# One access pattern for two, a stage buffer in other memory, and a planner with measured matmul times

## The chip, the cores and the metric

The kernel runs on one core of one Trainium2 chip. The metric is the device time of one execution in microseconds, lower is better; the time before is the median of three runs. A core has five engines that run instruction streams of their own: TensorE (PE in the profile; its weight loads are PEld), VectorE (DVE), ScalarE (ACT), GpSimd (POOL) and SyncE (SP), which here only issues transfers. Transfers between the on-chip memory (SBUF) and the chip's main memory (HBM) are moved by 16 DMA engines. Matmul results go to PSUM, which has eight banks.

## The reference

Two branches read the same kind of 2048 x 512 token matrix and are mixed by a gate for each token:

```
g = sigmoid(sum(u * gate_w))                     # one number per token
P = exp((A * dt) * l),  K = 2 * Re(sum_n C * dt * P)      # 512 channels, 128 states, 2048 positions
a = causal convolution of u with K over 2048 positions (by FFT of length 4096) + u * D_skip
b = ((x @ w_gate) * (x @ w_up)) @ w_down         # 512 -> 1792 -> 512, no other nonlinearity
out = g * a + (1 - g) * b
```

All of it is float32. The kernel writes each matmul of branch b as three products of two-part numbers (high and low part), which keeps float32 accuracy.

## The kernel before, in words

**Branch b (the GLU)** is the larger part of TensorE's work. The 1792 hidden features are 14 blocks of 128, taken in five groups; the 2048 tokens are four chunks of 512. For each group and chunk, `hidden` makes `pg` and `pu` (tokens times `w_gate` and `w_up`, 24 matmuls for a block: two tiles, four depth blocks, three parts), VectorE and ScalarE multiply them and split the result into `hh` and `hl`, and `down` multiplies by `w_down` into `y`. `evacuate` scales `y` by the gate and adds it to the output in HBM by accumulating transfers on GpSimd's queue. The token tiles `x` are split once, kept in HBM as `x_d` and loaded again for later groups.

**Branch a (the convolution)** goes by quarters of 128 channels. VectorE and ScalarE build tables for 32 channels at a time (16 blocks `b`); `k_block` turns a block into kernel values on TensorE (`k<-v,x`). After four blocks, `k_first` does the first stage of the transform of the kernel in two halves `h`: 16 to 48 matmuls into four PSUM banks (`k<-kt`), copies into two stage tiles and two 512 KB writes to the HBM array `s_d`. Then `transforms(q)`: `m_load` reads `s_d` back in another layout, `m_second`, `m_product` and `m_inverse` do the second stage, the product of the spectra and the first inverse stage, written to `y_d`, in four parts T; `m_last` reads `y_d` and does the last inverse stage (`k<-ev`), and `finish` gates the result and adds it to the output. For the last quarter (`q == KT - 1`) the tile is loaded by other code (`v<-y_d`), and the result of its last chunk is added on chip in `ends`.

`m_last` needs, for each of two halves of 16 columns, a tile of 128 partitions with 16 x 128 numbers each (8 KB): row `2k + c` of `y_d[q]` goes to partition `64c + k`. Before, two transfers do it, one for each c.

**Buffers.** Stage tiles come from the tag `ts` of the pool `mid`, three buffers of 4 KB a partition, given out in the order in which the plan asks. The tag `x` of the pool `tab` has two buffers of 8 KB a partition; it holds the tables of two blocks and, at the end, loaded inputs of the last quarter.

**The order of the work** is not that of the program text. Every piece is entered as a task with an engine, a planned duration in us, the tiles that it reads and writes, a rank and, for transfers, a size in KB (`dma=`). `Work.run` then simulates all engines: it always takes the task that can start first (on equal terms, the lower rank), gives out buffers when their last users end, and charges transfers to one bus at 320 KB per us (1024 is 3.2 us). The result is a fixed order of instructions for each engine. GLU products have rank 2, so they fill what the transforms leave. All instructions go through one wrapper, so the profile shows them all at line 102; tiles tell them apart.

Of the kernel before, what the change touches and what calls it, by code (L numbers as in the profile page):

```python
# [18 lines left out]
P = 128  # L19
L, D, N, F = 2048, 512, 128, 1792  # L20
KT = D // P
# [266 lines left out]
def gated_mix_kernel(  # L288
# [20 lines left out]
    add = work.add  # L309
# [224 lines left out]
    def product(pg, which, w, x, kt, after):  # L534
        base = which * D + kt * P

        def fn():
            for n, (a, b) in enumerate(THREE):
                pe.matmul(
                    pg.t, w[a].t[:, base : base + P], x.t[:, b * D : b * D + D], start=kt == 0 and n == 0, stop=kt == KT - 1 and n == 2  # L540
                )

        add("pe", 0.681, fn, r=[(w[0], which), (w[1], which), x], w=[pg], rank=2, after=after)

    steps = []

# [34 lines left out]
    def down(y, r, h, w, first, last):  # L581
        def fn():
            for n, (a, b) in enumerate(THREE):
                pe.matmul(
                    y.t, h[a].t[:, r * P : (r + 1) * P], w[b].t, start=first and n == 0, stop=last and n == 2
                )

        add("pe", 0.681, fn, r=[*h, *w], w=[y], rank=2)

    ending, stored = [], set()  # L590

# [106 lines left out]
    def u_part(c):  # L698
        ci, r0 = c // 2, c % 2
        ut = inp([P, 2, D])  # L700
        rows_u = uv.rearrange("p (c s r) d -> p c s r d", s=2, r=2)[:, ci, :, r0, :]
        add("sp", 0.42, lambda: sp.dma_start(ut.t, rows_u), w=[ut], dma=512, after=9.0 + 15.0 * c)
        fs = new("mid", "y", [P, 2, D], bufs=2)

        def score_of(j):
            r = 4 * ci + 2 * j + r0
            add(
                "dve", 0.77,
                lambda: dve.scalar_tensor_tensor(
                    fs.t[:, 0], ut.t[:, j, :], 1.0, gw[0].t[:, 2], op0=ALU.mult, op1=ALU.mult,  # L710
                    accum_out=score[:, r : r + 1],
                ),
                r=[ut, (gw[0], 2)], w=[(fs, 0), (m_gate, ("s", ci))], rank=0,
            )

        def fold(to, part, op):
            add(
                "dve", 0.69, lambda: dve.tensor_tensor(out=to(), in0=ut.t[:, 0], in1=ut.t[:, 1], op=op),
                r=[ut], w=[part], rank=0,
            )  # L720

        banks = [bank() for _ in range(4)]
        sts = [stage([P, 2, D]) for _ in range(2)]
        halves = [lambda: fs.t[:, 1], lambda: ut.t[:, 0]]

        def fn():
            for c, src in enumerate(halves):
                for g in range(4):
                    lanes = slice(32 * g, 32 * g + 32)
                    pe.matmul(  # L730
                        banks[g].t[64 * c : 64 * c + 64], w1_t[lanes, 64 * c : 64 * c + 64], src()[lanes],
                        start=True, stop=True, tile_position=(32 * g, 64 * c),
                    )

        for j in range(2):
            score_of(j)
        fold(halves[0], (fs, 1), ALU.add)
        fold(halves[1], (ut, 0), ALU.subtract)
        add("pe", 1.1, fn, r=[ut, fs, m_w1], w=banks, rank=1, hold=sts)
        for g in range(4):  # L740
            st, h, n2 = sts[g // 2], g % 2, 8 * g + c
            add("act", 0.59, lambda h=h, g=g, st=st: act.copy(st.t[:, h], banks[g].t), r=[banks[g]], w=[(st, h)])
            add(
                "pool", 1.7,
                lambda h=h, n2=n2, st=st: [
                    pool_q.dma_start(
                        s_d[:, :, c, n2, 0].rearrange("q k d -> k q d"),
                        st.t[64 * c : 64 * c + 64, h].rearrange("p (f d) -> p f d", f=KT),
                    )
                    for c in range(2)  # L750
                ],
                r=[(st, h)], w=[(m_su, n2)], dma=256,
            )
        if c % 2:
            cs = slice(4 * ci, 4 * ci + 4)
            sc, ga = (m_gate, ("s", ci)), (m_gate, ci)
            add("act", 1.5, lambda: act.activation(score[:, cs], score[:, cs], AF.Tanh, scale=0.5), r=[sc], w=[sc], rank=0)

            def gates():
                dve.tensor_scalar(ngate[:, cs], score[:, cs], -0.5, 0.5, op0=ALU.mult, op1=ALU.add)  # L760
                dve.tensor_scalar(gate[:, cs], score[:, cs], 0.5, 0.5, op0=ALU.mult, op1=ALU.add)

            add("dve", 0.4, gates, r=[sc], w=[ga], rank=0)
# [273 lines left out]
    def k_block(b, x, v):  # L1037
        pk = bank()

        def kgen():  # L1040
            pv = pk.t.rearrange("p (g j) -> p g j", j=64)
            for d in range(TB):
                ch, g = d % 4, d // 4
                for c in range(2):
                    pe.matmul(
                        pv[32 * ch : 32 * ch + 32, g, :], x.t[:, c, d, :], v.t[:, c, d, :], start=c == 0, stop=c == 1,
                        tile_position=(0, 32 * ch),
                    )

        if b % 4 == 0:  # L1050
            kts["now"] = new("tab", "kt", [P, 64, 32])
        kt, g0 = kts["now"], b % 4 * 8
        add("pe", 2.15, kgen, r=[x, v], w=[pk], rank=0, hold=[kt], many=True)
        add(
            "act", 1.09,
            lambda: act.copy(
                kt.t[:, :, g0 : g0 + 8].rearrange("p n g -> p g n"), pk.t.rearrange("p (g j) -> p g j", j=64)
            ),
            r=[pk], w=[(kt, b % 4)],
        )  # L1060
        if b % 4 == 3:
            k_first(b // 4, kt)

    def k_first(q, kt):

        tt(0.19, lambda: kt.t[:, 48, :], lambda: kt.t[:, 48, :], lambda: skip[:, q], ALU.add, [m_skip], [kt])
        for h in range(2):
            banks, sts = [bank() for _ in range(4)], [stage([P, 8, 4, 32]) for _ in range(2)]

            def fn(h=h, banks=banks):  # L1070

                to = 0
                for first, n, second in K_COLS[h]:
                    for b in range(2):
                        n0 = (first, second)[b]
                        for c in range(4):
                            lanes = slice(32 * c, 32 * c + 32)
                            pe.matmul(
                                banks[c].t[:, 32 * to : 32 * (to + n)], w1k_t[lanes, b],
                                kt.t[lanes, n0 : n0 + n, :].rearrange("p n g -> p (n g)"),  # L1080
                                start=b == 0, stop=b == 1, tile_position=(32 * c, 0),
                            )
                    to += n

            add("pe", 2.08, fn, r=[kt, m_w1k], w=banks, rank=-1, hold=sts)
            for half in range(2):

                st = sts[half]
                for c in range(4):
                    cs = slice(256 * half, 256 * half + 256)  # L1090
                    evict(
                        q, c, 0.4, lambda c=c, st=st: st.t[:, :, c, :],
                        lambda c=c, banks=banks, cs=cs: banks[c].t[:, cs].rearrange("p (n g) -> p n g", g=32),
                        [banks[c]], [(st, c)],
                    )
                n0 = 16 * h + 8 * half
                add(
                    "sp", 0.42,
                    lambda n0=n0, st=st: sp.dma_start(
                        s_d[q].rearrange("k c n u d -> (k c) n u d")[:, n0 : n0 + 8, 1],  # L1100
                        st.t.rearrange("p n c g -> p n (c g)"),
                    ),
                    r=[st], w=[(m_sk, (q, n0))], dma=512,
                )

    def evict(q, n, us, to, src, r, w):
# [51 lines left out]
    def m_second(q, ins, w):  # L1158
# [18 lines left out]
                            )  # L1177

        src = [(t, k) for t, k, _ in ins]
        add("pe", 1.85, fn, r=[*src, w], w=banks[0] + banks[1], rank=1, hold=[to])  # L1180
        for i in range(2):
            for e in range(2):
                bk = banks[i][e]
# [40 lines left out]
    def m_inverse(q, T0, ys, ws):  # L1224
# [14 lines left out]
                                    ys[t].t[lanes, k, i, e], start=k == 0, stop=k == 1, tile_position=(32 * j, 64 * e),  # L1239
                                )  # L1240

        add("pe", 2.13, fn, r=[*ys, *(w for w, _ in ws)], w=banks, rank=1, hold=sts, many=True)
        for j in range(4):
            st, m = sts[j // 2], j % 2
            evict(
# [16 lines left out]
    def m_last(q):  # L1262
# [3 lines left out]
        for half in range(2):  # L1266
# [6 lines left out]
            if end:  # L1273
# [2 lines left out]
            t = new("mid", "ev", [P, 16, P], bufs=2)  # L1276
            rows_y = y_d[q].rearrange("(k c) (h n) d -> h c k (n d)", c=2, h=2)[half]
            add(
                "sp", 0.84,
                lambda t=t, rows_y=rows_y: [  # L1280
                    sp.dma_start(t.t[64 * c : 64 * c + 64].rearrange("p n d -> p (n d)"), rows_y[c]) for c in range(2)
                ],
                r=[(m_y, (q, T)) for T in range(4)], w=[t], dma=1024,
            )
            src.append(t)
            rhs.append(lambda t=t: t.t)
# [11 lines left out]
                            start=True, stop=True, tile_position=(64 * c, 32 * g),  # L1298
                        )

        add("pe", 1.6, fn, r=src, w=banks[0] + banks[1], rank=1, hold=fins[0] + fins[1])
        for half in range(2):
            finish(q, half, banks[half], fins[half])

# [170 lines left out]
```

## Time and profile before

| | |
|---|---|
| median of 3 runs | 618.01 us (614.53 to 618.51) |
| profiled execution, its own time | 617.16 us |
| span of the profile | 615.4 us |
| mean granted TensorE clock | 0.991 |
| TensorE busy | 594.9 us (97%) |
| VectorE busy | 514.4 us (84%) |
| ScalarE busy | 405.8 us (66%) |
| transfers | 136.22 MB, mean 221 GB/s |

In the profile's groups, `k<-ev,w_t` is an output tile and the two inputs of a matmul; `x32` counts instructions. In the chain that ended last each row is start, length and what ran or was waited for. In a table by stages the columns are the stretch, its length, the busy time and count of PE, PEld, DVE, ACT and POOL, then the granted clock, the busy share of the 16 DMA engines and GB/s. In a list of transfers each row has the tiles, the queue, how often, the size of one, and the median time from issue to landing.

### The profile page before, as it was taken

Reading aid. Unit: us, or ns where it says so; the run is one execution under the profiler, and the core shown is the slowest. Engines: PE = TensorE matmul, PEld = TensorE weight load, DVE = VectorE, ACT = ScalarE, POOL = GpSimd, SP = SyncE. Lnnn points to the kernel's source line nnn. Section 1 sums busy time; section 2 is a strip of 40 time slices with the busy share of each in tenths; the row PEclk is TensorE's granted clock in tenths of the full one; section 3 lists DMA queues with packets and bytes.
Section 4 is the critical chain, followed back from the end, with each engine's and each line's share of the span. In section 5 each row is a group of like instructions: output and inputs, shape, how many; then the busy total and the mean of one; then the engine's idle time right before and its main releaser. Section 6 shows DMA issues by size and latency. Waiting matters only on the chain.

```text
span 615.4 us, 16233 instructions
## 1 busy us (share of the span) xinstructions
PE 594.9 (97%) x6628; PEld 454.8 (74%) x6628; DVE 514.4 (84%) x813; ACT 405.8 (66%) x923; POOL 106.4 (17%) x165
## 2 busy tenths in 40 slices
PE   8989999999899999999999999899999999999993
PEld 5767777777778877787777788568877787777772
DVE  6967999999989999999999999785999972547725
ACT  5568868776778778678789748575796463464320
POOL 0153433331221102020121011120101011130201
PEclk9999999999999999999999999899999999999997
DMA  8699968657968979399999869397888569798956
GB/s 266 183 359 308 300 235 299 185 138 216 272 183 209 274 249 276 120 257 251 292 207 230 227 209 211 78 191 156 249 225 240 178 180 240 208 289 199 214 131 120
DMA packets 102223, 136.22 MB, mean 221 GB/s; under 512 B 7300, under 2 KB 68228, under 8 KB 101124
## 3 DMA queue, kind: packets, MB, share of 16 engines
q1 hardware_dynamic: 80788, 100.57, 53.0%
q0 software_dynamic: 20672, 34.35, 27.4%
q8 instruction: 52, 0.85, 0.5%
q10 hardware_dynamic: 688, 0.26, 0.2%
q14 instruction: 23, 0.19, 0.1%
HBM read 77.75 MB, written 57.41 MB: 220 GB/s over the span
## 4 chain that ended last, share of the span: by engine, by line
PE 84%; DVE 7%; DMA 4%; issue 2%; ACT 2%; DVEq 0%; SPq 0%; ACTq 0%
PE pg L102 22%; PE pu L102 22%; PE y L102 21%; PE k L102 18%; DMA in<-in_u 2%; DVE x L102 2%; DMA x<-x_d 1%; DVE v L102 1%; DVE y L102 1%; DMA ev<-in_wts 1%; DVE ts L102 1%; ACT acc L102 1%; DMA out<-acc 0%; DVE hl L102 0%; DVE h L102 0%
## 5 line engine op out<-in xcount | busy, mean ns | idle before, releaser
L102 PE MATMUL pg<-x,whi 128*128 128x512 f32 x440 | 137.5, 392 | 1.0 <-ACT whi L102 0.9
L102 PE MATMUL pu<-x,whi 128*128 128x512 f32 x440 | 137.0, 391 | 0.0
L102 POOL DMA_DIRECT2D out<-acc x52 | 44.6, 917 | 331.7 <-ACT acc L102 300.5
L102 PEld LDWEIGHTS pg<-x,whi 128*128 128x128 f32 x440 | 82.9, 188 | 19.8 <-ACT whi L102 2.4
L102 PEld LDWEIGHTS pu<-x,whi 128*128 128x128 f32 x440 | 82.9, 188 | 18.9 <-issue 1.9
L102 PE MATMUL y<-dhi,hl 128*128 128x512 f32 x224 | 91.1, 407 | 0.7 <-ACT acc L102 0.4
L102 PE MATMUL pg<-x,wlo 128*128 128x512 f32 x220 | 88.1, 401 | 1.8 <-DMA x<-x_d 1.1
L102 PE MATMUL pu<-x,wlo 128*128 128x512 f32 x220 | 87.9, 400 | 1.6 <-issue 1.6
L102 PE MATMUL y<-dlo,hh 128*128 128x512 f32 x224 | 87.6, 391 | 0.0
L102 PE MATMUL y<-dhi,hh 128*128 128x512 f32 x224 | 87.4, 390 | 0.0
L102 DVE TENSOR_TENSOR h<-pu,h 128x512 f32<-128x512 f32 x55 | 37.9, 689 | 36.1 <-PE pu L102 32.0
L102 ACT CAST hh<-h 128x512 fp32r<-128x512 f32 x56 | 34.8, 621 | 42.8 <-DVE h L102 42.6
L102 ACT ACTIVATE acc<-y,ngate 128x512 f32<-128x512 f32 x68 | 46.0, 688 | 25.6 <-PE y L102 19.3
L102 ACT COPY ts<-k 128x512 f32<-128x512 f32 (+1 forms) x116 | 48.4, 503 | 21.4 <-PE k L102 21.4
L102 ACT COPY h<-pg 128x512 f32<-128x512 f32 x55 | 32.4, 589 | 42.5 <-PE pg L102 29.5
L102 PEld LDWEIGHTS y<-dhi,hl 128*128 128x128 f32 x224 | 42.0, 187 | 21.9 <-issue 7.7
L102 PEld LDWEIGHTS pg<-x,wlo 128*128 128x128 f32 x220 | 41.4, 188 | 17.6 <-issue 4.3
L102 PEld LDWEIGHTS pu<-x,wlo 128*128 128x128 f32 x220 | 41.4, 188 | 14.2 <-issue 4.9
L102 PEld LDWEIGHTS y<-dhi,hh 128*128 128x128 f32 x224 | 42.1, 188 | 9.3
L102 PEld LDWEIGHTS y<-dlo,hh 128*128 128x128 f32 x224 | 42.1, 188 | 7.6
L102 POOL DMA_DIRECT2D s_d<-ts x64 | 39.6, 626 | 36.0 <-ACT ts L102 28.1
L102 DVE TENSOR_TENSOR hl<-h,hh 128x512 fp32r<-128x512 f32 x56 | 38.4, 686 | 5.0 <-ACT hh L102 4.8
(115 smaller groups left out, 1011.9 us busy)
## 6 DMA issues: line engine op xcount, KB each, us to landing
x<-x_d SPq DMA_DIRECT2D x32, 512.0 KB, 6.5
out<-acc POOLq DMA_DIRECT2D x52, 256.0 KB, 6.4
in<-s_d SPq DMA_DIRECT2D x24, 512.0 KB, 6.1
raw<-in_wts SPq DMA_DIRECT2D x36, 256.0 KB, 4.3
x_d<-x POOLq DMA_DIRECT2D x16, 512.0 KB, 6.4
s_d<-ts POOLq DMA_DIRECT2D x64, 128.0 KB, 5.7
s_d<-ts SPq DMA_DIRECT2D x16, 512.0 KB, 5.9
y_d<-ts SPq DMA_DIRECT2D x16, 512.0 KB, 6.3
```

What stands on the lines that cost most here:

```text
L102: got = getattr(self.engine, name)(*args, **kw)
```

## The change

It does three things.

- In `m_last`, the two 64-partition transfers of one tile become one transfer into all 128 partitions. The planned size goes from 1024 to 1200 and the planned issue time from 0.84 to 0.42 us.
- In `k_first`, the second half of the last quarter stages its copies in one tile of the tag `x` (the two halves of it in place of two `ts` tiles).
- Planned durations of TensorE tasks change; the instructions in them do not.

```diff
-        add("pe", 0.681, fn, r=[(w[0], which), (w[1], which), x], w=[pg], rank=2, after=after)
+        add("pe", 0.684, fn, r=[(w[0], which), (w[1], which), x], w=[pg], rank=2, after=after)
...
-        add("pe", 0.681, fn, r=[*h, *w], w=[y], rank=2)
+        add("pe", 0.684, fn, r=[*h, *w], w=[y], rank=2)
...
-        add("pe", 1.1, fn, r=[ut, fs, m_w1], w=banks, rank=1, hold=sts)
+        add("pe", 1.26, fn, r=[ut, fs, m_w1], w=banks, rank=1, hold=sts)
...
-        add("pe", 2.15, kgen, r=[x, v], w=[pk], rank=0, hold=[kt], many=True)
+        add("pe", 2.24, kgen, r=[x, v], w=[pk], rank=0, hold=[kt], many=True)
...
-            banks, sts = [bank() for _ in range(4)], [stage([P, 8, 4, 32]) for _ in range(2)]
+            banks = [bank() for _ in range(4)]
+            if h and q == KT - 1:
+                pair = new("tab", "x", [P, 2, 8, 4, 32], bufs=2)
+                sts = [((pair, i), lambda i=i: pair.t[:, i]) for i in range(2)]
+            else:
+                sts = [(st, lambda st=st: st.t) for st in (stage([P, 8, 4, 32]) for _ in range(2))]
...
-            add("pe", 2.08, fn, r=[kt, m_w1k], w=banks, rank=-1, hold=sts)
+            add("pe", 2.17, fn, r=[kt, m_w1k], w=banks, rank=-1, hold=[st for st, _ in sts])
...
-                st = sts[half]
+                st, st_at = sts[half]
+                piece = lambda c, st=st: (st, c) if not isinstance(st, tuple) else (st[0], (st[1], c))
...
-                    r=[st], w=[(m_sk, (q, n0))], dma=512,
+                    r=[piece(c) for c in range(4)], w=[(m_sk, (q, n0))], dma=512,
...
-        add("pe", 1.85, fn, r=[*src, w], w=banks[0] + banks[1], rank=1, hold=[to])
+        add("pe", 2.11, fn, r=[*src, w], w=banks[0] + banks[1], rank=1, hold=[to])
...
-        add("pe", 2.13, fn, r=[*ys, *(w for w, _ in ws)], w=banks, rank=1, hold=sts, many=True)
+        add("pe", 2.25, fn, r=[*ys, *(w for w, _ in ws)], w=banks, rank=1, hold=sts, many=True)
...
             rows_y = y_d[q].rearrange("(k c) (h n) d -> h c k (n d)", c=2, h=2)[half]
             add(
-                "sp", 0.84,
-                lambda t=t, rows_y=rows_y: [
-                    sp.dma_start(t.t[64 * c : 64 * c + 64].rearrange("p n d -> p (n d)"), rows_y[c]) for c in range(2)
-                ],
-                r=[(m_y, (q, T)) for T in range(4)], w=[t], dma=1024,
+                "sp", 0.42,
+                lambda t=t, rows_y=rows_y: sp.dma_start(t.t.rearrange("p n d -> p (n d)"), rows_y),
+                r=[(m_y, (q, T)) for T in range(4)], w=[t], dma=1200,
             )
...
-        add("pe", 1.6, fn, r=src, w=banks[0] + banks[1], rank=1, hold=fins[0] + fins[1])
+        add("pe", 2.12, fn, r=src, w=banks[0] + banks[1], rank=1, hold=fins[0] + fins[1])
```

More of the change, by code (lines that the diff above doesn't have):

```diff
@@ L1091, in k_first @@
                     evict(
-                        q, c, 0.4, lambda c=c, st=st: st.t[:, :, c, :],
+                        q, c, 0.4, lambda c=c, st_at=st_at: st_at()[:, :, c, :],
                         lambda c=c, banks=banks, cs=cs: banks[c].t[:, cs].rearrange("p (n g) -> p n g", g=32),
-                        [banks[c]], [(st, c)],
+                        [banks[c]], [piece(c)],
                     )
@@ L1098, in k_first @@
                     "sp", 0.42,
-                    lambda n0=n0, st=st: sp.dma_start(
+                    lambda n0=n0, st_at=st_at: sp.dma_start(
                         s_d[q].rearrange("k c n u d -> (k c) n u d")[:, n0 : n0 + 8, 1],
-                        st.t.rearrange("p n c g -> p n (c g)"),
+                        st_at().rearrange("p n c g -> p n (c g)"),
                     ),
-                    r=[st], w=[(m_sk, (q, n0))], dma=512,
+                    r=[piece(c) for c in range(4)], w=[(m_sk, (q, n0))], dma=512,
                 )
```

## The prediction

> **What bounds the kernel now.** I read the page first, engine shares and the forty slices, then the summary of the chain that ended last.
>
> ```profile
> span 615.4 us, 16233 instructions
> ...
> PE 594.9 (97%) x6628; PEld 454.8 (74%) x6628; DVE 514.4 (84%) x813; ACT 405.8 (66%) x923; POOL 106.4 (17%) x165
> ...
> PE   8989999999899999999999999899999999999993
> ...
> DMA packets 102223, 136.22 MB, mean 221 GB/s; under 512 B 7300, under 2 KB 68228, under 8 KB 101124
> ...
> PE 84%; DVE 7%; DMA 4%; issue 2%; ACT 2%; DVEq 0%; SPq 0%; ACTq 0%
> ```
>
> TensorE is busy 594.9 of 615.4 us and makes up 84% of the chain. It runs its instructions in one fixed order, so whatever its next instruction waits for is paid nearly in full: there is almost no idle time to take it back from. Only 20.5 us are idle. The table by stages says where half of that is:
>
> ```profile
> 600.00:606.00 6.00, 5.17 (x22) 3.62 (x20) 5.79 (x10) 0.59 (x1) 2.24 (x2) 1.00 0.02 1
> 606.00:612.00 6.00, 0.00 (x0) 0.00 (x0) 2.32 (x7) 0.00 (x0) 0.63 (x1) 0.66 1.31 213
> 612.00:615.40 3.40, 0.00 (x0) 0.00 (x0) 0.00 (x0) 0.00 (x0) 0.00 (x0) 0.50 0.49 166
> ```
>
> 9.4 us at the end and some 0.8 us before it are a tail of VectorE and stores. The other 10 us are spread over the start and the middle.
>
> **The change, part by part.**
>
> *The plan's constants.* No instruction changes. Seven TensorE costs rise: 656 products by 0.003 us, then 8 by 0.16, 16 by 0.09, 8 by 0.09, 16 by 0.26, 8 by 0.12 and 4 by 0.52, together 12.6 us that the plan did not know of. They change only the order in which work is issued. The gain is at most the 10 us of idle above; a loss of the same size is possible. I take 0, between -4 and +8.
>
> *The second half of the last kernel stage.* Before, it needs two of three "ts" buffers, and the first half still holds two of them until its writes have landed. The chain and the SP queue in that stretch:
>
> ```profile
> 509.03 1.93 PE k L102 x16
> ...
> 526.15 1.97 PE k L102 x48
> ...
> 534.49 1.88 PE k L102 x32
> ```
> ```profile
> 511.85 7.31 SPq L102 DMA_DIRECT2D s_d<-ts  x2
> ...
> 529.00 1.33 SPq L102 DMA_DIRECT2D s_d<-ts  x2
> ...
> 534.91 0.93 SPq L102 DMA_DIRECT2D v<-s_d  x2
> ```
>
> The halves are 17.1 us apart on TensorE, and GLU products fill the gap. With table buffers the second half can follow as soon as the first half's four banks are copied out, some 13 us earlier. Its two writes still go down the same transfer queue as everything before them. At the rate of that stretch (500 to 545), two 512 KB writes are 4.3 us, so the loads of the last stage could start some 4 us earlier, not 13. TensorE is full until 605, so this can only shorten the tail:
>
> ```profile
> DMA packets 10313, 10.88 MB, mean 242 GB/s; under 512 B 451, under 2 KB 8053, under 8 KB 10054
> ```
>
> ```profile
> 604.93 0.39 PE L102 MATMUL y<-dhi,hh 128*128 128x512 f32 x1
> ...
> 606.45 3.67 SPq L102 DMA_DIRECT2D out<-kt  x4
> 606.95 1.40 DVE L102 SCALAR_TENSOR_TENSOR kt<-y,ngate,kt 128x512 f32<-128x512 f32 x2
> ```
> ```profile
> out<-kt SPq DMA_DIRECT2D x4, 256.0 KB, 5.3
> ```
>
> If the transforms finish 4 us before the last product, the last store needs 605.3, one product of 0.7 us, an issue of 0.4 us and 5.3 us of landing. That is 611.7, and 612.4 with a little at the close: 3 us less than now. The new tile sits between two users of the same two "x" buffers; the last load into that slot reads what the tile's own write has stored, so it waits for nothing new.
>
> *The loads of the inverse stage.* `m_last` for the first three quarters loads two tiles, each by two 64-partition transfers of 512 KB; now each is one transfer of 1 MB. Twelve issues become six, and the queue of SP, which is not the bound, saves six issues of about half a us. The price lies elsewhere. The source keeps the order c, k, row: its slowest dimension is c, of size **2**, over 64 strided rows, while the destination has 128 partitions. The transfers it replaces had 64 rows outermost on both sides. Does a transfer's slowest dimension decide how many of the 16 engines it uses? Before has one transfer with a slow dimension under 16, a constant of four partitions, and the view of transfers has no landing time for it:
>
> ```profile
> ri<-in_w SPq DMA_DIRECT2D x1, 512.0 KB
> ...
> ev<-in_rows SPq DMA_DIRECT2D x1, 256.0 KB
> ...
> w1k_t<-in_w1k SPq DMA_DIRECT2D x1, 128.0 KB, 4.4
> skip<-in_dsk SPq DMA_DIRECT2D x1, 2.0 KB
> ```
>
> Landings are found by counting sixteen completion marks for each transfer on a semaphore. These rows without a time share one semaphore, and its marks in the trace do not come out: 549 for 35 transfers, that is 34 times 16 and 5. The five belong to the constant: one mark about 1.1 us after its issue and four at its end. All other semaphores give exactly 16 each. So four rows outermost left work on four engines, and two blocks outermost against 128 partitions should leave it on **two**.
>
> The Trainium skill ("DMA: Bandwidth & Descriptors", "Why a DMA increments its semaphore by 16 and not by 1") states this rule: the engines used are the largest number up to 16 that divides the slowest dimension above 1 of both sides, and the lowest-numbered ones are taken. The marks of the constant agree with it; no run here yet shows it for a large load. By its figure of about 27 GiB/s for one engine ("Specifications") one load would take an estimated 18 us.
>
> What would a load on two engines take? Both ends come from rates of all sixteen. The densest slice near the end moves 430 GB/s, 26.9 for one engine:
>
> ```profile
> GB/s 214 430 207 119 257 298 333 300 129 17 0 237 309 164 218 218 18 0 0 27 0 0 0 0 0 0 0 0 9 143 176 183 170 288 286 312 377 105 0 0
> ```
>
> 1.048 MB on two engines then takes 19.5 us. Both loads of a pair have the same shape, so I put them on the same two engines: 39 (no row shows which engines a transfer takes; on four different ones a pair would be through in some 22 us, and the sum below would be +10). The mean of the page, 221 GB/s or 13.8 an engine, gives 38 and 76. I take the fast end, since behind such a pair most else is waiting, plus 3 us for the accumulating stores that share those engines by the other queue: **42 us**. Nothing at all (16 engines) is the bound on the other side.
>
> Who waits? First the matmuls of `m_last` themselves, then on TensorE everything behind them. On SP's queue, transfers of all later tiles also need their share of those two engines. That its transfers stand in line shows in the stretch 500 to 545, where the writes to s_d took 13.6 us behind these very loads, against 5.9 on the page:
>
> ```profile
> ev<-y_d SPq DMA_DIRECT2D x4, 512.0 KB, 11.7
> s_d<-ts SPq DMA_DIRECT2D x4, 512.0 KB, 13.6
> ```
> ```profile
> s_d<-ts SPq DMA_DIRECT2D x16, 512.0 KB, 5.9
> ```
>
> The three places, first issues of SP's queue, then the chain around the matmuls that read these loads:
>
> ```profile
> 276.48 2.84 SPq L102 DMA_DIRECT2D ev<-y_d  x4
> 286.14 1.48 SPq L102 DMA_DIRECT2D s_d<-ts  x2
> ...
> 289.92 3.04 SPq L102 DMA_DIRECT2D x<-x_d  x4
> ...
> 375.36 2.40 SPq L102 DMA_DIRECT2D ev<-y_d  x4
> ...
> 507.36 1.89 SPq L102 DMA_DIRECT2D ev<-y_d  x2
> ```
> ```profile
> 302.49 1.88 PE k L102 x32
> 304.37 2.26 PE y L102 x9
> 306.63 2.72 PE pg L102 x12
> ...
> 386.69 0.97 PE k L102 x2
> 387.67 2.33 issue
> 390.00 3.31 PE k L102 x30
> ```
>
> - First quarter: issue 276.5, 2 us until data moves, 42 for the pair: 320.5. The matmuls stand at 302.5, so TensorE waits 18 us. Two writes and the four x loads lie behind (3 MB, some 7 us), and x is wanted 4.1 us after the matmuls' start: 3 more. **21**.
> - Second quarter: 375.4 + 44 = 419.4. Already now TensorE stops between the second and third matmul of this group, and the rest starts at 390.0; with the pair late it starts at 419.4. **29**.
> - Third quarter: issue 507.4 into a full queue (half of the 11.7 us above, 6) + 42 = 555.4, against 534.5: 21, and up to 31 if the freed "ts" buffers let the plan put these matmuls earlier. **24**. The writes of the last kernel stage stand behind the same pair and land about 25 us later too, which this wait covers; of the 3 us at the tail I keep 1.
>
> The last quarter loads its tile by other code and is untouched. Sum: 21 + 29 + 24 - 1 + 0 = 73 us. The profiled execution took 617.16 us for its span of 615.4, 0.9 us under the median of 618.01, so 617.2 + 73 = **690 us**.
>
> With 39 and 76 us in place of 42, the same sum gives 681 and about 790, the upper end only if two engines with others idle run no faster than sixteen together.
>
> **The rivals.**
>
> *Sixteen engines after all, shorter tail: 614 us.* If the access pattern reaches the engines with a dimension of 64 or 128 outermost, the pair takes what the four halves take now, or a little less: 4 transfers of 512 KB with a median landing of 11.7 us. Then only the tail's 3 us are left, 617.2 - 3 = 614, with the order worth -4 to +3 on top. It decides wherever the new transfer leaves sixteen marks. For it: the same bytes, the same 8 KB rows on both sides. Against it: the slow dimension in the diff and the constant's five marks. This is the case on the other side, not slower than before.
>
> In its favour the Trainium skill ("DMA: Bandwidth & Descriptors", "Rules for kernel authors") tells authors not to split a load into partition halves and to use one 128-partition transfer; by that, nothing is lost here. The same table warns of a small outermost dimension, so it does not decide.
>
> *Sixteen engines, and the new order starves TensorE: 625 us.* The old constants made TensorE later than planned, which left slack for copies and loads. Exact ones place each matmul at the planned arrival of its data. Where it arrives late, TensorE stops, and the second-quarter case shows the price: 2.33 us of standing plus 1.4 us for 30 matmuls that took 3.31 instead of about 1.9 us. Three such stops, less the tail, give 617.2 + 11 - 3 = 625. For it: this stop exists already. Against it: the plan now charges these loads 1200 instead of 1024, so it expects them later.
>
> **How the numbers follow.** Two engines 0.75, sixteen with a shorter tail 0.17, sixteen with stops 0.08. The first has its own range of 665 to 735; rate and placement are unknown in it. For 8 in 10 the second must come in as well, so the range is 612 to 735. A difference of 1% (6 us) is what a measurement of this kernel can tell from none, since its own three runs span 614.53 to 618.51. Faster by over 1% (under 611.8) keeps 0.04, out of the second case; within 1%, 0.14; slower 0.82.
>
> **What would show it.** Each `ev<-y_d` of 1 MB with 20 to 45 us to landing, or, if only two engines mark their end, many transfer rows with no landing time at all; three stops of TensorE of 18 to 30 us ahead of `k<-ev`, with the granted clock at half in them; low GB/s in those stretches; and x loads landing late behind them. Right for the staging: the second `k<-kt` group of the last stage within 5 us of the first. Wrong: six loads landing in under 12 us, TensorE still at 97%, and a span near 612.

## The result, and the profile after

The changed kernel takes 699.69 us (median of 4 runs, 698.01 to 700.89) against 616.27 us before (median of 4): the ratio is 1.1354, with a 95% interval of 1.1293 to 1.1414. The prediction said 690 us. The kernel before was timed again beside each set of runs below (medians of 615.25 to 615.88 us). Times are medians of all runs, while a ratio compares means and leaves out runs over 1.5% above the fastest of their kernel, so the two can differ by a few tenths of a per cent.

The page of the changed kernel, first its engine shares, then the slices and the granted clock, then the chain that ended last:

```profile
span 698.1 us, 16198 instructions
...
PE 606.5 (87%) x6628; PEld 461.6 (66%) x6628; DVE 513.0 (73%) x813; ACT 405.6 (58%) x923; POOL 106.4 (15%) x165
...
PE   8989999999999999085999997099999816999897
...
PEclk9999999999999999687999999599999956999999
...
PE 57%; DMA 22%; issue 10%; DVE 7%; ACT 3%; POOL 0%; SPq 0%; DVEq 0%; ACTq 0%; POOLq 0%
```

The same 6628 matmuls, but three holes in TensorE's row, and in each of them and just behind it a lower clock. In the chain, DMA grew from 4% to 22%. Idle time of TensorE rose from 20.5 us (615.4 - 594.9) to 91.6 (698.1 - 606.5), which is 71.1 of the 82.7 us between the spans. The other 11.6 us are busy time: the same matmuls took longer.

TensorE's own timeline, each stop with the idle time and what ended it in brackets:

```profile
298.15 0.79 PE L102 MATMUL pg<-x,wlo 128*128 128x512 f32 x1 [17.30 <-DMA x<-x_d]
...
322.73 3.56 PE L102 MATMUL k<-v,x 128*32 128x64 f32 x124 [9.39 <-ACT ts L102]
...
454.28 2.03 PE L102 MATMUL k<-v,x 128*32 128x64 f32 x66 [23.22 <-ACT ts L102]
...
562.15 2.08 PE L102 MATMUL k<-ev,w_t 64*32 64x512 f32 x16 [7.02 <-DMA ev<-y_d]
...
582.34 1.96 PE L102 MATMUL k<-ev,w_t 64*32 64x512 f32 x16 [18.11 <-DMA ev<-y_d]
```

Five stops in three places: 26.7, 23.2 and 25.1 us, 75.0 in all. Only the last two stand ahead of the matmuls that read the new loads. The others come one or two steps further down: the first waits for an `x` tile whose load was issued between the two new ones. Who waited for whom, by total, names the link to the next two (each row: us in total, number of waits, the longest):

```profile
ACT ts L102 <- DMA s_d<-ts: 33.9, 2, 23.9
...
PE k L102 <- ACT ts L102: 32.6, 2, 23.2
...
PE k L102 <- DMA ev<-y_d: 25.1, 2, 18.1
```

ScalarE could not copy into a `ts` buffer until an older write from it had landed, and TensorE waited for the bank that ScalarE was to empty. SP's queue around the first two loads shows why that write was late:

```profile
265.44 0.55 SPq L102 DMA_DIRECT2D ev<-y_d  x1
266.04 3.78 SPq L102 DMA_DIRECT2D x<-x_d  x3
269.91 4.91 SPq L102 DMA_DIRECT2D ev<-y_d  x1
274.87 22.26 SPq L102 DMA_DIRECT2D pb<-par_d  x2
297.23 26.67 SPq L102 DMA_DIRECT2D s_d<-ts  x4
```

Two small loads of 64 KB took 22 us to *issue* (the first alone 21.8). No semaphore that this first load waits for was updated near the end of its issue, so it was the queue itself that stood, and the writes to `s_d` behind them were not only slow to move but late to be issued. The list of transfers has what the prediction looked for:

```profile
s_d<-ts SPq DMA_DIRECT2D x14, 512.0 KB, 15.8
ev<-y_d SPq DMA_DIRECT2D x6, 1024.0 KB
```

No landing time stands beside the six loads. In the trace's events each left three completion marks where an ordinary transfer leaves sixteen: one 0.9 to 1.5 us after its issue began (5.3 us for the load whose issue itself took 4.9), two at its end. With these counts the landings can be read off: the second load of each pair lands 50.6, 50.5 and 42.6 us after its own issue, the first 31.4, 31.1 and 22.9. The second lands 23.7, 19.9 and 20.3 us after the first, near the 19.5 us that the prediction worked out for one load on two engines.

The marks of the transfers around a pair tell more. The x load issued at 266.0 us left fourteen of its sixteen marks at 269.1 to 272.4 and the last two at 297.1 and 298.1, just behind the landing of the first new load at 296.9. The `pb` load issued at 274.9 left fourteen at 297.9 to 298.1 and two at 319.7 and 320.7; the second new load landed at 320.6. The load of weights behind the third pair left fourteen at 560.3 to 561.1 and two at 582.2 and 582.9, with the second new load landing at 582.3. So both loads of a pair lay on the same two engines, one after the other, and a transfer behind them could not land before its share on these two was through, however long the other fourteen had been done.

Stretches around the first, third and last stop (columns as in the tables above; the granted clock is the third number from the right):

```profile
280.85:298.15 17.30, 0.00 (x1) 0.01 (x1) 4.20 (x5) 3.37 (x5) 0.84 (x1) 0.56 0.33 76
298.15:303.50 5.35, 5.35 (x13) 4.07 (x14) 0.00 (x0) 2.37 (x4) 0.00 (x0) 0.50 0.15 60
...
431.06:454.28 23.22, 0.00 (x2) 0.00 (x1) 3.50 (x4) 0.42 (x2) 0.00 (x0) 0.55 0.30 95
454.28:457.10 2.82, 2.82 (x108) 2.82 (x112) 0.00 (x0) 1.52 (x4) 0.00 (x0) 0.50 1.05 345
...
564.20:582.34 18.14, 0.03 (x5) 0.00 (x0) 0.00 (x0) 0.00 (x0) 0.00 (x0) 0.50 0.30 100
582.34:586.80 4.46, 4.46 (x22) 2.31 (x23) 2.87 (x5) 2.34 (x5) 0.00 (x0) 0.50 0.70 210
...
694.20:698.10 3.90, 0.00 (x0) 0.00 (x0) 0.75 (x1) 0.00 (x0) 0.00 (x0) 1.00 0.27 99
```

While the loads hold the queue, 76 to 100 GB/s move, and for 2.8 to 5.4 us after each of these stops TensorE works at half clock. The last row is the tail: 3.9 us from the last matmul to the end, where before had 10.1.

### The profile page after: what moved, and what is told of

It is laid out like the page before. It is cut to its first block, busy times and chain, and to the rows that moved or that the text cites. A ratio compares the mean times of both kernels' runs of the same rounds, so it can differ in the third digit from the quotient of the medians.

```text
span 698.1 us, 16198 instructions
## 1 busy us (share of the span) xinstructions
PE 606.5 (87%) x6628; PEld 461.6 (66%) x6628; DVE 513.0 (73%) x813; ACT 405.6 (58%) x923; POOL 106.4 (15%) x165
## 4 chain that ended last, share of the span: by engine, by line
PE 57%; DMA 22%; issue 10%; DVE 7%; ACT 3%; POOL 0%; SPq 0%; DVEq 0%; ACTq 0%; POOLq 0%
PE pg L102 15%; PE pu L102 15%; PE y L102 13%; PE k L102 13%; DMA ev<-y_d 6%; DMA x<-x_d 4%; DMA s_d<-ts 4%; DMA y_d<-ts 3%; DMA out<-acc 2%; DVE x L102 2%; DVE v L102 2%; DMA raw<-in_xT 1%; ACT ts L102 1%; DMA v<-y_d 1%; DMA ev<-in_wts 1%
## 5 line engine op out<-in xcount | busy, mean ns | idle before, releaser
L102 PE MATMUL pg<-x,whi 128*128 128x512 f32 x440 | 139.4, 397 | 0.7 <-ACT whi L102 0.7
L102 PE MATMUL pu<-x,whi 128*128 128x512 f32 x440 | 138.7, 395 | 0.0
L102 PE MATMUL pg<-x,wlo 128*128 128x512 f32 x220 | 89.1, 405 | 19.9 <-DMA x<-x_d 17.3
L102 PEld LDWEIGHTS pg<-x,whi 128*128 128x128 f32 x440 | 84.5, 192 | 19.8 <-ACT whi L102 2.3
L102 PE MATMUL pu<-x,wlo 128*128 128x512 f32 x220 | 89.8, 408 | 0.0
L102 PE MATMUL k<-v,x 128*32 128x64 f32 x2048 | 36.3, 231 | 33.2 <-ACT ts L102 32.6
L102 PEld LDWEIGHTS k<-v,x 128*32 128x32 f32 x2048 | 33.5, 115 | 39.2 <-ACT ts L102 33.8
L102 PEld LDWEIGHTS y<-dhi,hl 128*128 128x128 f32 x224 | 42.0, 187 | 19.9 <-issue 5.9
```

The lines of the kernel that those rows point to most:

```text
L102: got = getattr(self.engine, name)(*args, **kw)
```

## The experiments

The theory: a source whose slowest dimension is 2 leaves the load on two of sixteen engines; everything else follows from its lateness. The main rival: the plan's new figures and buffers order the work so that TensorE starves.

**The load alone, in the order of before.**

```diff
 # kernel before, m_last; planned 0.84 us and 1024 kept
-  [sp.dma_start(t.t[64 * c : 64 * c + 64]..., rows_y[c]) for c in range(2)]
+  sp.dma_start(t.t.rearrange("p n d -> p (n d)"), rows_y)
```

> The kernel before with only the new access pattern: planned figures of these loads stay at 0.84 us and 1024, so every engine's order is that of before, except that SP issues 6 transfers in place of 12. Theory (a slowest dimension of 2 leaves the load on two engines): each tile's load leaves 3 completion marks, a pair takes 42 to 55 us, TensorE stops three times for about 75 us in all and runs some 12 us longer at the half clock after the stops: 690 to 705 us. Rival (the new order of the plan makes the time): 617 us as before.

Measured: 700.81 us, ratio 1.1395 (1.1337 to 1.1452). The pattern alone gives the whole loss, in an order that is the old one instruction for instruction on TensorE, VectorE and ScalarE. TensorE's waits:

```profile
PE k L102 <- DMA ev<-y_d: 30.5, 2, 18.9
PE y L102 <- DVE hl L102: 26.6, 1, 26.6
PE k L102 <- DVE v L102: 25.7, 1, 25.7
```

82.8 us in four waits, against 75.0 in the changed kernel and in other places: the order decides where the lateness surfaces, and its sum less. Each load left three marks, and the pairs landed 42.8, 46.0 and 45.2 us after the issue of their second load. The time lies within the expectation, but its terms do not: the stops are 8 us longer, and of the 12 us for the half clock only 3.3 appeared as busy time (598.2 against 594.9):

```profile
PE 598.2 (86%) x6628; PEld 456.8 (65%) x6628; DVE 514.3 (74%) x813; ACT 405.5 (58%) x923; POOL 106.4 (15%) x165
```

The two errors nearly cancel, which is luck.

**The number of engines.** In the changed kernel, the rows are cut into more blocks, so that only the slowest dimension differs; the bytes, the 8 KB rows and the order of every engine stay.

```diff
-  rows_y = y_d[q].rearrange("(k c) (h n) d -> h c k (n d)", c=2, h=2)[half]
+  rows_y = y_d[q].rearrange("(k c) (h n) d -> h c k (n d)", c=16, h=2)[half]     # also 8, 4
```

> The changed kernel with 16 in place of 2 as the number of blocks c of these loads, so the slowest dimension is 16, over 8 strided rows; every engine's order is that of the changed kernel. The rows land on other partitions, so a part of the convolution's output is not the reference's. Theory: 16 engines, 16 marks, landing in 6 to 12 us, no stop above 3 us ahead of these matmuls, 609 to 615 us. Rival (one strided transfer of 1 MB is slow in itself): 699 us, as changed. Rival (order): 699 us.

> As the run with 16 blocks, with 8 (rows land on other partitions too). Theory: eight engines, 9 marks, 1 MB at 8 x 26.9 GB/s is 4.9 us and the pair 10 us alone, some 13 to 16 with what stands beside it; 611 to 622 us. Rivals: 699 us.

> As the runs with 16 and 8 blocks, with 4 (rows land on other partitions, so a part of the output is not the reference's). Theory: four engines, 5 marks, 1 MB at 4 x 26.9 GB/s is 9.7 us, the pair 19.5 alone and 22 to 30 with what stands beside it: 635 to 665 us. The run with 8 gave 631.7, with 2 699.7.

| slowest dimension | completion marks of one load | second load of a pair lands after (us, three pairs) | time (us) | ratio to before |
|---|---|---|---|---|
| 2 (the change) | 3 | 50.6, 50.5, 42.6 | 699.69 | 1.1354 (1.1293 to 1.1414) |
| 4 | 5 | 39.7, 31.7, 28.5 | 654.78 | 1.0645 (1.0572 to 1.0719) |
| 8 | 9 | 30.3, 22.8, 21.1 | 631.69 | 1.0260 (1.0213 to 1.0307) |
| 16 | 16 | 16.7, 16.6, 13.7 | 620.36 | 1.0079 (1.0050 to 1.0109) |

Below sixteen blocks the marks are one soon after the issue and, at the end, one for each engine. The transfers of the run with 16 blocks have a landing time in the list again:

```profile
ev<-y_d SPq DMA_DIRECT2D x6, 1024.0 KB, 13.7
```

Time falls with each doubling by 44.9, 23.1 and 11.3 us, each about half the one before, as it would be if the loss went as one over the number of engines. That settles the mechanism: not the size of 1 MB, not the stride, but the count of engines. (The time for 4 blocks rests on two runs.) The loads took longer than expected throughout: 28.5 to 39.7 us against 22 to 30 with 4 blocks, 21.1 to 30.3 against 13 to 16 with 8, and with 16 the second of a pair 13.7 to 16.7 against 6 to 12. Other transfers stand on the same queue; that they are the reason was not tested. The time with 4 blocks is within its expectation, with 8 it is 10 us above the 622, and with 16 it missed my 609 to 615 us by 5 us, which the next two runs explain.

**Everything but the load.**

```diff
 # changed kernel, m_last
-  "sp", 0.42,
-  lambda t=t, rows_y=rows_y: sp.dma_start(t.t.rearrange("p n d -> p (n d)"), rows_y),
-  ... dma=1200,
+  "sp", 0.84,
+  ... [sp.dma_start(t.t[64 * c : 64 * c + 64]..., rows_y[c]) for c in range(2)],
+  ... dma=1024,
```

> The changed kernel with only the loads taken back (two transfers of 64 partitions, planned 0.84 us and 1024); constants and staging stay as changed. Theory: 609 to 615 us, a tail after the last matmul of about 4 to 7 us instead of 10. Rival (order): 690 us or more. Rival (sixteen engines, but exact constants starve TensorE): 620 to 630 us.

Measured: 612.70 us, ratio 0.9955 (0.9929 to 0.9981), the lowest median of all versions. Constants and staging together gain 0.45%, 2.8 us: little, but its interval excludes 1. Page, then the last stretches:

```profile
PE 593.3 (98%) x6628; PEld 452.5 (74%) x6628; DVE 513.6 (85%) x813; ACT 405.9 (67%) x923; POOL 106.4 (18%) x165
...
PEclk9999999999999999999999999999999999999999
```
```profile
595.00:603.40 8.40, 8.23 (x35) 5.94 (x33) 3.98 (x7) 0.62 (x1) 0.00 (x0) 1.00 0.22 81
603.40:607.50 4.10, 0.00 (x0) 0.00 (x0) 0.75 (x1) 0.00 (x0) 0.00 (x0) 0.90 0.25 93
```

The tail is 4.1 us long, the clock never drops before the end, and there is no stop like the one at 390 us. That last point is no merit of the change: the run with the staging alone (below) still has the order of before in that stretch, and there the same matmuls stopped for 0.44 us in place of 2.33:

```profile
389.51 1.95 PE L102 MATMUL k<-ev,w_t 64*32 64x512 f32 x30 [0.44 <-issue]
```

So that stop differs from one execution to another.

**The order of the change with two loads.**

```diff
 # changed kernel, m_last; planned 0.42 us and 1200 kept
-  lambda t=t, rows_y=rows_y: sp.dma_start(t.t.rearrange("p n d -> p (n d)"), rows_y),
+  ... [sp.dma_start(t.t[64 * c : 64 * c + 64]..., rows_y[c]) for c in range(2)],
```

> The changed kernel with its planned figures for these loads kept (0.42 us, 1200), so every engine's order is that of the changed kernel, but with two transfers of 64 partitions for each tile. It separates what was left in the run with 16 blocks (620.4 us against 612.7 us with two loads planned as before). If the transfer of strided rows itself costs it: 611 to 614 us. If the order that the figures 0.42 and 1200 give costs it: 618 to 622 us.

Measured: 619.87 us, ratio 1.0070 (1.0041 to 1.0099), the same as with one transfer on sixteen engines (620.36). So that transfer costs nothing in itself, and the order that the figures 0.42 and 1200 give costs 7.2 us against that of 0.84 and 1024. Little of it is a stop: in the two profiled executions, the slowest of one version and the fastest of the other (spans 619.5 and 607.5), TensorE was busy 600.5 us in place of 593.3, and idle 19.0 in place of 14.2. Why the same matmuls took longer in that order, no run shows. Two sister runs set one figure each:

> Changed kernel with two loads for each tile, planned issue 0.84 us as before and planned size 1200 as changed. With 0.84 and 1024 the run gave 612.7 us, with 0.42 and 1200 619.9 us. If the size makes that difference: 618 to 621 us. If the issue time makes it: 611 to 615 us. If neither does, and any new order falls somewhere between 611 and 621: no prediction from the figures is possible, and this run and its sister will not add up.

> As the sister run with the figures the other way round: issue 0.42 us as changed, size 1024 as before. If the issue time makes the difference of 7 us: 618 to 621 us. If the size makes it: 611 to 615 us.

Measured: 614.66 us (ratio 0.9994, 0.9964 to 1.0024) with 0.84 and 1200, and 619.07 us (1.0038, 0.9998 to 1.0079) with 0.42 and 1024. The medians lean towards the issue time of 0.42 us, but the second run spread from 611.9 to 623.2 us and the intervals overlap. Which figure does it stays open.

**Each other part alone.**

The kernel before gets the seven TensorE constants of the change and nothing else.

> The kernel before with the seven TensorE constants of the change alone. The prediction put their effect between -4 and +8 us, with 0 as the value. With two loads, staging and constants together the run gave 612.7 us against 615.9: if the constants carry that gain, 611 to 614 us; if the staging carries it, 615 to 618 us. Theory: a part of the gain lies in the middle (the stop at 390 us is gone), so I expect 613 to 616 us.

Measured: 615.14 us against 615.46, ratio 1.0011 (0.9984 to 1.0038): nothing that can be told. The time is within the expectation, its reason (the stop at 390 us) is not the one.

Then the kernel before gets the staging alone: the second half of the last kernel stage goes to a tile of the tag `x`.

> The kernel before with only the second half of the last kernel stage staged in the table tiles. Prediction: 3 us less by a shorter tail, 612 to 614 us, the second group of these matmuls within 6 us of the first instead of 17, and some 6 to 7 us between the last matmul and the end instead of 10. Rival (TensorE is full, the tail is set by the last product and store alone): 616 us.

Measured: 614.05 us, ratio 0.9983 (0.9948 to 1.0018): nothing that can be told. In its chain the second half now follows the first by 4.2 us, and in SP's queue the loads of the last stage start at 527.1 in place of 534.9; yet its tail is still 9.4 us, where 6 to 7 was expected:

```profile
505.86 1.93 PE k L102 x16
...
510.06 1.97 PE k L102 x48
```
```profile
527.14 2.01 SPq L102 DMA_DIRECT2D v<-s_d  x4
```
```profile
602.20:611.60 9.40, 0.02 (x1) 0.00 (x0) 2.27 (x7) 0.00 (x0) 0.59 (x1) 0.62 1.02 196
```

The staging does what it says, and the tail does not follow from it. The last matmuls of the transforms show why. Here they are before, then with the staging alone, then with the constants alone:

```profile
597.26 1.95 PE L102 MATMUL k<-v,w_t 64*32 64x512 f32 x32
```
```profile
593.47 1.95 PE L102 MATMUL k<-v,w_t 64*32 64x512 f32 x32
```
```profile
580.94 2.94 PE L102 MATMUL k<-v,w_t 64*32 64x512 f32 x32
```

Before, they end 6.1 us ahead of TensorE's last matmul, with the staging 6.8, with the constants 25.9. In the first two, VectorE's work on their results (`ts`) lasts to TensorE's end or past it (606.1 against 605.3, and 602.3 against 602.2), and the last additions and stores come behind that. The order that the constants give puts them far ahead, and every run with the constants has a short tail: 4.3 us with the constants alone (last matmul at 609.8 of a span of 614.1 us), 3.9 to 4.1 in the others. With the constants alone three stops of 1.2 to 2.2 us ahead of the last quarter's matmuls (`k<-v,w2s`, `k<-x,e`), 4.8 us in all, took back most of that.

## Why the prediction was right

- **Engines by the slowest dimension**: right, and now shown: three marks for each load, and the row of four runs. The Trainium skill ("DMA: Bandwidth & Descriptors", "Why a DMA increments its semaphore by 16 and not by 1") has this rule; the marks of 4, 8 and 16 blocks agree with it. By its figure of about 27 GiB/s for one engine ("Specifications") a load would take an estimated 18 us; the shortest here took 22.9 us from its issue, and the second of a pair 19.9 to 23.7 us from the landing of the first.
- **The pair, 42 us from the start of its data**: measured 55, 51 and 43 us from the first issue to the last mark in the changed kernel, where the prediction had 44, 44 and 48 with the time until data moves. It was short by 7 to 11 us in the first two places, where x loads and accumulating stores were issued around the pair, and 5 us too long in the third; what each of these neighbours cost, no run separates. The choice of the same two engines for both loads of a pair, and the share of them that every transfer behind the pair was said to need, are shown by the fourteen early and two late marks. The slow end, 76, was far off.
- **The three stops, 21 + 29 + 24 = 74 us**: measured 26.7 + 23.2 + 25.1 = 75.0. The sum is better than its terms deserve: the terms assumed the places of before, and in the changed kernel two of the three lie on x loads and `ts` buffers.
- **A missing term: the half clock after a stop.** The prediction counted it in a rival and not in its own sum. Against the run of the same order with two loads, TensorE was busy 606.5 us in place of 600.5, 6.0 us more. Idle time rose by 72.6 (91.6 against 19.0). The two are the 78.6 us between these spans. That the clock makes the 6.0 us is the reading of two pairs: here TensorE was busy at half clock for 22.7 us against 3.4, and in the run of the load alone in the order of before for 12.1 against 2.8, with 3.3 us more busy time.

```profile
span 619.5 us, 16211 instructions
...
PE 600.5 (97%) x6628; PEld 455.7 (74%) x6628; DVE 512.4 (83%) x813; ACT 404.6 (65%) x923; POOL 106.4 (17%) x165
```

- **The order, taken as 0**: on sixteen engines or with two loads the new order costs 0.7% (4.4 us), within the stated -4 to +8, although it has the shorter tail. So the sum of 73 us is answered, in the profiles, by 82.7: 72.6 of idle time where the sum had 74, 6.0 of clock where it had nothing, and 4.1 between the spans of 619.5 and 615.4 where it had -1 for tail and order together. That is the 9.7 us between 690 and 699.69.
- **The tail, -1 of a possible -3**: 3.9 us instead of 10.1 in the changed kernel, so -6. The reason given was wrong: the staging alone moved the loads of the last stage 7.8 us earlier and gave no shorter tail, and the constants alone, which the working gave no part in the tail, had one of 4.3 us.
- **The rival of 614 us** for sixteen engines was 6 us too low: 620.36. It had the tail, allowed the order -4 to +3, and did not weigh what the plan's figures for the load do to it. The rival of 625 us named the order, though not as three stops of 3.7 us: in the run with 16 blocks no stop of TensorE is longer than 2.3 us. Its price came from the stop at 390 us, which the run with the staging alone shows at 0.44 us in the same order.

## What to carry to other kernels

Before two transfers are joined, look at the slowest dimension of *both* sides: a split of 128 partitions by a small outer factor in the source (2, 4 and 8 here) left the load on as many engines, and the queue behind it paid as well. Missing landing times, or completion counts that are no multiple of 16, showed it here at once. A part of a change that gains a few us can be kept when another part of it loses eighty: here the version with the two loads put back takes 0.45% less than before, and only runs of single parts showed it. A planner's figure is part of the kernel: two numbers for one transfer moved this one by 7 us through the order alone, with the same instructions.

## What the runs showed of the hardware that I had not expected

A load on two engines held the *issue* of later transfers on its queue, not only the shares of their data on these two engines: two loads of 64 KB stood 22.3 us at SP in the changed kernel, and the fourteen other engines got their shares only after that. And the granted clock fell to 0.50 within each long stop and stayed there 2.8 to 5.4 us after work resumed, 6.0 us of extra busy time in all against the run of the same order. One strided transfer of 1 MB on sixteen engines, on the other hand, was worth the same as two of half the partitions: 620.36 against 619.87 us.
